# Squares in two 64-row tiles, two block rows at a time, and weight stacks in three column tiles

## The chip, the cores and the metric

The kernel runs on one core of one Trainium2 chip. The metric is device time in microseconds (us), the median of several executions. TensorE multiplies matrices and writes to the memory PSUM; VectorE and ScalarE work element by element and copy results out of PSUM; SyncE issues the transfers (DMA). "Before" drifts from chip to chip and run to run: its medians beside the different experiments were 2007.0, 2006.6, 2003.6, 2008.3 and 2000.6 us, and within the rounds of e1 to e4 its runs lie anywhere from 1998 to 2008 us. So small differences are judged by ratios within the same rounds, or by single stretches of the traces.

## The reference

A small attention block makes x from 32 inducing points; a SwiGLU FFN with an rms norm in front follows.

```python
def mab(q, kv):                       # softmax(q kv^T / sqrt(C)) kv
    ...
h = mab(I, x); y = mab(x, h)          # B=4, N=12416, m=32, C=128
rms = sqrt(mean(y*y, -1) + 1e-06)     # per row of 128
xn = y / rms * rms_g
out = (silu(xn @ w_gate) * (xn @ w_val)) @ w_out    # d_ff = 1536
```

All is float32. y = a @ h has rank 32, so the kernel never feeds y to the FFN: it multiplies the 32 attention weights `a`, scaled by 1/rms, with the "stacks" h*g*w_gate and h*g*w_val. y itself is made only to get its mean square. "a" and the stacks are each split into a rounded high part and what the rounding left, the low part: 32 rows of "a" go in as high, low, high, low against high, high, low, low of the stack, so one matmul with 128 rows sums all four products.

## The kernel before

Rows come in 97 blocks of 128 per batch. Four blocks are a unit (25 units a batch, counted from 0; the last two have three and two blocks), four units are a set. The FFN of one unit is 12 steps j. Into these steps the kernel weaves, by a fixed plan, the attention of the next batch ("attention steps") and the "seam" of a later set: transposes, squares, scale, split. Everything shares the PSUM tiles "mm", of which there are two.

```python
ps_gv = pool("ps_gv", 4, space=PSUM)
ps_acc = pool("ps_acc", 2, space=PSUM)
ps_m = pool("ps_m", 2, space=PSUM)          # the tiles "mm"
...
def square(t, rows, at):                    # one block row t of a set: 4 blocks
    k = rows // m
    ps = ps_m.tile([P, R, C], F32, name="mm", tag="mm")
    nc.tensor.matmul(ps[:, 0:k, :], st["aT"][0:rows, ts(t, P)], diag[b][0:rows, 0:k, :], ...)   # L437
    sq = work.tile([P, R, C], F32, name="sq", tag="sq")
    nc.scalar.activation(sq[:, 0:k, :], ps[:, 0:k, :], AF.Square)
    nc.vector.reduce_sum(out=st["ms"][:, ds(at // m, k)], in_=sq[:, 0:k, :], axis=AX.X)
...
def stack(i, c):                            # h*g*w, 512 columns at a time
    ps = bank()
    nc.tensor.matmul(ps[:], st["hg"][:], st.pop(("w", i, c))[:], ...)                           # L392
    ... VectorE: high part to all rows, low part to rows 64 to 127
...
for j in range(NJ):                         # ffn of one unit
    matmul g (L504); matmul v (L506); silu on ScalarE; multiply on VectorE
    if j == 4 and stores:
        stores.pop()()                      # turn_out of the unit before: transposes, copy L494, store
    slot(j)                                 # attention steps, then the seam's steps planned here
    if len(late) > 1:
        late.pop(0)()                       # project (L487) of two steps earlier
```

`diag` holds four copies of h in a block-diagonal form, so one float32 matmul with 128 rows and 512 columns gives y for four blocks; three quarters of the array's work are zeros.

Of the kernel before, what the change touches and what calls it, by code (L numbers as in the profile page):

```python
# [9 lines left out]
F32 = mybir.dt.float32  # L10
F32R = mybir.dt.float32r
I32 = mybir.dt.int32
U32 = mybir.dt.uint32
AF = mybir.ActivationFunctionType
ALU = mybir.AluOpType
AX = mybir.AxisListType
PSUM = bass.MemoryType.PSUM

P = 128
R = 4  # L20
TB = 4
GB = R * TB
# [3 lines left out]
def kernel(  # L26
# [27 lines left out]
    nc = tc.nc  # L54
    B, N, C = x.shape
    m = inducing.shape[0]
    F = moe_w_gate.shape[1]
    NB = N // P
    NJ = F // P
    NG = NB // GB  # L60
    H = P // 2
    SCALE = float(1.0 / (C ** 0.5))
    assert C == P and m * R == P and F % 512 == 0 and N % P == 0
    assert NG >= 1 and NB - NG * GB in (0, 1)


    groups = [(g * GB, GB, R, TB) for g in range(NG)]
# [15 lines left out]
    def chunks(s):  # L83

        at = 0
        for t in range(TB):
            rows = m * sum(units[u][1] > t for u in sets[s])
            if rows:
                yield t, rows, at
            at += rows  # L90
# [12 lines left out]
    def first(s):  # L103
        return units[sets[s][0]][0]

    def count(s):
        return sum(units[u][1] for u in sets[s])

    def pool(name, bufs, **kw):
        return ctx.enter_context(tc.tile_pool(name=name, bufs=bufs, **kw))  # L110
# [5 lines left out]
    small = pool("small", 2)  # L116
    work = pool("work", 3)
    once = pool("once", 1)
# [7 lines left out]
    ps_m = pool("ps_m", 2, space=PSUM)  # L126
# [15 lines left out]
    gam = const.tile([P, 1], F32, name="gam")  # L142
# [6 lines left out]
    w32 = [[dram.tile([P, 512], F32, name=f"w{i}{c}") for c in range(F // 512)] for i in range(2)]  # L149
# [14 lines left out]
    ps = ps_m.tile([P, 512], F32, name="mm", tag="mm")  # L164
# [54 lines left out]
    sc, diag, stacks = {}, {}, {}  # L219

    def attention(b, load_next):

        st = {}
        steps = []
        add = steps.append
# [7 lines left out]
        def bank():  # L233
            if b:
                return ps_m.tile([P, 512], F32, name="mm", tag="mm")
            return ps_gv.tile([P, 512], F32, name="gv", tag="gv")
# [99 lines left out]
        def end_h():  # L336
            ps = bank()
            nc.tensor.matmul(ps[:, 0:C + 1], fold[:].rearrange("p q m -> p (q m)"), st["hl"][:], start=True, stop=True)
            rec = small.tile([P, 1], F32, name="rec")
            nc.vector.tensor_scalar_add(out=rec[:], in0=ps[:, C:C + 1], scalar1=1e-9)  # L340
            nc.vector.reciprocal(out=rec[:], in_=rec[:])
            h = st["h"] = once.tile([P, C], F32, name="h")
            nc.vector.tensor_scalar_mul(out=h[:], in0=ps[:, 0:C], scalar1=rec[:])

            d = diag[b] = small.tile([P, R, C], F32, name="diag")
            nc.gpsimd.memset(d[:], 0.0)
            for q in range(R):
                nc.gpsimd.tensor_copy(out=d[ts(q, m), q, :], in_=h[ts(q, m), :])

        def turn_h():  # L350
            ps = bank()
            nc.tensor.transpose(ps[:, 0:P], st["h"][:], ident[:])
            hT = st["hT"] = once.tile([P, m], F32, name="hT")
            nc.vector.tensor_copy(out=hT[:], in_=ps[:, 0:m])
            hg = st["hg"] = once.tile([P, P], F32, name="hg")
            nc.vector.tensor_scalar_mul(out=hg[:], in0=ps[:, 0:P], scalar1=gam[:])
            stacks[b] = [stk.tile([P, F], F32R, name=n) for n in ("sg", "sv")]

        add(end_h)
# [22 lines left out]
        def exp2():  # L382
            nc.scalar.activation(sc[b][:, 0:NB * m], sc[b][:, 0:NB * m], AF.Exp, scale=SCALE)

        def fetch(i, c):
            w = st["w", i, c] = work.tile([P, 512], F32, name="w", tag="sq")
            nc.sync.dma_start(out=w[:], in_=w32[i][c][:])

        def stack(i, c):

            ps = bank()
            nc.tensor.matmul(ps[:], st["hg"][:], st.pop(("w", i, c))[:], start=True, stop=True)  # L392
            w = stacks[b][i]
            nc.vector.tensor_copy(out=w[:, ts(c, 512)], in_=ps[:])
            nc.vector.tensor_tensor(out=w[H:P, ts(c, 512)], in0=ps[H:P, :], in1=w[H:P, ts(c, 512)].bitcast(F32),
                                    op=ALU.subtract)

        for s in range(len(sets)):
            add(lambda s=s: scores2(s))
# [1 line left out]
                add(lambda s=s: turn_s(s - 1))  # L401
        add(lambda: turn_s(len(sets) - 1))
        add(exp2)
        ics = [(i, c) for c in range(F // 512) for i in range(2)]
        add(lambda: fetch(*ics[0]))
        for one, two in zip(ics, ics[1:]):
            add(lambda one=one, two=two: (fetch(*two), stack(*one)))
        add(lambda: stack(*ics[-1]))
        return steps

    def blocks(b, s):

        return sc[b][:, ds(first(s) * m, count(s) * m)].rearrange("p (j m) -> p j m", m=m)

    def seam(b, s):

        st = {}
        nb = count(s)

        def turn_a():  # L420
            ps = ps_m.tile([P, 512], F32, name="mm", tag="mm")
            for t, rows, at in chunks(s):
                nc.tensor.transpose(ps[0:rows, ts(t, P)], sc[b][:, ds(first(s) * m + at, rows)], ident[:])  # L423
            aT = st["aT"] = once.tile([P, 512], F32, name="aT")
            for r0, r1, n in rects(s):
                nc.scalar.copy(out=aT[r0:r1, 0:n], in_=ps[r0:r1, 0:n])  # L426
            l = st["l"] = small.tile([P, GB], F32, name="l")
            nc.vector.reduce_sum(out=l[:, 0:nb], in_=blocks(b, s), axis=AX.X)
            nc.vector.tensor_scalar_add(out=l[:, 0:nb], in0=l[:, 0:nb], scalar1=1e-9)
            nc.vector.scalar_tensor_tensor(out=l[:, 0:nb], in0=l[:, 0:nb], scalar=1e-6, in1=l[:, 0:nb],  # L430
                                           op0=ALU.mult, op1=ALU.mult)
            st["ms"] = small.tile([P, GB], F32, name="ms")

        def square(t, rows, at):
            k = rows // m
            ps = ps_m.tile([P, R, C], F32, name="mm", tag="mm")
            nc.tensor.matmul(ps[:, 0:k, :], st["aT"][0:rows, ts(t, P)], diag[b][0:rows, 0:k, :], start=True, stop=True)  # L437
            sq = work.tile([P, R, C], F32, name="sq", tag="sq")
            nc.scalar.activation(sq[:, 0:k, :], ps[:, 0:k, :], AF.Square)  # L439
            nc.vector.reduce_sum(out=st["ms"][:, ds(at // m, k)], in_=sq[:, 0:k, :], axis=AX.X)  # L440

        def scale():
            ms = st["ms"]
            nc.vector.scalar_tensor_tensor(out=ms[:, 0:nb], in0=ms[:, 0:nb], scalar=1.0 / C, in1=st["l"][:, 0:nb],  # L444
                                           op0=ALU.mult, op1=ALU.add)
            rs = small.tile([P, GB], F32, name="rs")
            nc.gpsimd.tensor_tensor(out=rs[:, 0:nb], in0=ms[:, 0:nb], in1=mhalf[:, 0:nb], op=ALU.pow)  # L447
            a = blocks(b, s)
            nc.gpsimd.tensor_tensor(out=a, in0=a, in1=rs[:, 0:nb].unsqueeze(2).to_broadcast((P, nb, m)), op=ALU.mult)

        def split():
            ps = ps_m.tile([P, 512], F32, name="mm", tag="mm")
            for t, rows, at in chunks(s):
                nc.tensor.transpose(ps[0:rows, ts(t, P)], sc[b][:, ds(first(s) * m + at, rows)], ident[:])  # L454
            tag = "" if len(sets[s]) == R else "s"
            hi, lo = (halves.tile([P if not tag else rects(s)[0][1], rects(s)[0][2]], F32R, name=n + tag) for n in ("hi", "lo"))
            for r0, r1, n in rects(s):
                nc.vector.tensor_copy(out=hi[r0:r1, 0:n], in_=ps[r0:r1, 0:n])
                nc.vector.tensor_tensor(out=lo[r0:r1, 0:n], in0=ps[r0:r1, 0:n], in1=hi[r0:r1, 0:n].bitcast(F32),
                                        op=ALU.subtract)  # L460
            for q, u in enumerate(sets[s]):
                split_of[b, u] = (q, hi, lo)

        return [turn_a] + [lambda c=c: square(*c) for c in chunks(s)] + [scale, split]

    split_of, moving = {}, {}

# [64 lines left out]
    for k, (b, s) in enumerate(order):  # L532
        if len(sets[s]) < R:
            continue
        following = order[k + 1:k + 3]
        if following and len(sets[following[0][1]]) < R:
            steps = seam(*following.pop(0))
            for i, f in enumerate(steps):
                plan.setdefault((b, sets[s][0], min(NJ - 1, 2 * i + 1)), []).append(f)
        if following:  # L540
            steps = seam(*following[0])
            at = [(1, 1), (1, 4), (1, 7), (1, 10), (2, 1), (2, 4), (2, 10)]
            for (n, j), f in zip(at, steps):
                plan.setdefault((b, sets[s][n], j), []).append(f)
    after = {}
# [52 lines left out]
```

## Time and profile before

| what | value |
|---|---|
| median of 3 runs | 2007.02 us |
| FFN begins | 149.3 us |

### The profile page before, as it was taken

The numbers are of one execution on the slowest core, as the hardware profiler recorded it, in microseconds if no ns is written. First come the engines' busy times: TensorE is split into PE (matmuls) and PEld (weight loads), VectorE is DVE, ScalarE is ACT, GpSimd is POOL, SyncE is SP. The second block draws the span as 40 slices with busy tenths as digits, with TensorE's granted clock in tenths as the row PEclk, the third lists the DMA queues.
The fourth block names the chain that finished last, engine by engine and source line by source line (L and its number), as shares of the span: only waits on it lengthen the run. The fifth ranks groups of instructions, "written<-read, shape, count | busy, mean of one in ns | idle before, by whom it ended". The sixth has DMA issues, their size and how long they took to land.

```text
span 2004.2 us, 22358 instructions
## 1 busy us (share of the span) xinstructions
PE 1910.3 (95%) x7445; PEld 1101.8 (55%) x7445; DVE 1170.0 (58%) x1973; ACT 910.5 (45%) x1550; POOL 116.7 (6%) x92
## 2 busy tenths in 40 slices
PE   4369999999999999999999999999999999999999
PEld 2135555555556555555556655555555655555556
DVE  3655565565756555556666656556575556556555
ACT  1114445445445444544544544544544544444544
POOL 0110000010000000000000000001000000000000
PEclk7589999999999999999999999999999999999999
DMA  5240110410201101130111010000020110111010
GB/s 185 68 167 19 33 30 19 137 44 27 64 27 29 32 22 32 59 123 22 47 38 32 25 32 29 25 28 21 27 64 27 30 32 28 36 32 32 27 33 24
DMA packets 44707, 90.35 MB, mean 45 GB/s; under 512 B 9232, under 2 KB 13360, under 8 KB 41520
## 3 DMA queue, kind: packets, MB, share of 16 engines
q1 hardware_dynamic: 44400, 88.90, 14.3%
q8 instruction: 59, 0.97, 0.2%
q14 instruction: 56, 0.46, 0.1%
q10 hardware_dynamic: 192, 0.02, 0.0%
HBM read 36.45 MB, written 27.00 MB: 32 GB/s over the span
## 4 chain that ended last, share of the span: by engine, by line
PE 91%; DVE 2%; ACT 2%; issue 1%; DMA 0%; POOL 0%; SPq 0%; ACTq 0%; POOLq 0%; DVEq 0%
PE acc L487 50%; PE gv L506 13%; PE gv L504 13%; PE mm L437 4%; PE mm L492 2%; PE mm L242 2%; PE mm L366 1%; PE mm L320 1%; PE mm L250 1%; PE mm L392 1%; PE mm L454 1%; PE mm L423 1%; ACT L508 0%; PE mm L308 0%; PE mm L375 0%
## 5 line engine op out<-in xcount | busy, mean ns | idle before, releaser
L510 DVE TENSOR_TENSOR u<-silu,gv 128x512 f32<-128x512 f32 (+2 forms) x1200 | 804.1, 671 | 707.1 <-ACT silu L508 605.5
L487 PE MATMUL acc<-u,wo 128*128 128x512 f32 (+2 forms) x2400 | 1206.1, 584 | 0.0
L508 ACT ACTIVATE silu<-gv 128x512 f32<-128x512 f32 (+2 forms) x1200 | 701.5, 585 | 836.6 <-PE gv L504 454.0
L504 PE MATMUL gv<-a,sg 128*128 128x512 f32 (+2 forms) x1200 | 930.4, 775 | 20.0 <-ACT silu L508 15.3
L487 PEld LDWEIGHTS acc<-u,wo 128*128 128x128 f32 x2400 | 426.0, 189 | 151.6 <-issue 85.9
L506 PE MATMUL gv<-a,sv 128*128 128x512 f32 (+2 forms) x1200 | 466.2, 389 | 0.0
L504 PEld LDWEIGHTS gv<-a,sg 128*128 128x128 f32 x1200 | 228.0, 190 | 298.2 <-issue 216.8
L506 PEld LDWEIGHTS gv<-a,sv 128*128 128x128 f32 x1200 | 228.7, 191 | 274.2 <-issue 197.6
L447 POOL TENSOR_TENSOR rs<-ms,mhalf 128x16 f32<-128x16 f32 (+2 forms) x28 | 71.8, 2564 | 1567.7 <-DVE ms L444 1567.7
L437 PE MATMUL mm<-diag,aT 128*128 128x512 f32 (+1 forms) x208 | 102.1, 574 | 0.8 <-ACT aT L426 0.8
L440 DVE TENSOR_REDUCE ms<-sq 128x4 f32<-128x512 f32 (+1 forms) x104 | 67.2, 649 | 39.0 <-ACT sq L439 38.7
L439 ACT ACTIVATE sq<-mm 128x512 f32<-128x512 f32 (+1 forms) x104 | 59.2, 569 | 57.3 <-PE mm L437 56.3
L499 ACT COPY oT<-acc 128x512 f32<-128x512 f32 (+2 forms) x100 | 57.3, 573 | 52.1 <-PE acc L487 51.8
L494 DVE COPY o<-mm 128x512 f32<-128x512 f32 (+2 forms) x100 | 66.8, 668 | 1.7 <-PE mm L492 1.7
L492 PE MATMUL mm<-ident,oT 128*128 128x128 f32 x388 | 58.6, 272 | 0.5 <-ACT oT L499 0.5
L492 PEld LDWEIGHTS mm<-ident,oT 128*128 128x128 f32 x388 | 48.2, 140 | 13.3 <-ACT oT L499 0.9
L242 PE MATMUL mm<-ident,xn 128*128 128x128 f32 x288 | 43.1, 272 | 0.0
L437 PEld LDWEIGHTS mm<-diag,aT 128*128 128x128 f32 (+1 forms) x208 | 36.4, 192 | 11.4 <-issue 4.9
L250 PE MATMUL gv<-xT,indT 128*32 128x512 f32 (+1 forms) x50 | 16.8, 889 | 27.0 <-DVE xT L215 25.7
L242 PEld LDWEIGHTS mm<-ident,xn 128*128 128x128 f32 x288 | 35.8, 140 | 9.3
L242 PE MATMUL gv<-ident,xn 128*128 128x128 f32 x96 | 20.4, 382 | 17.6 <-DVE xT L215 14.8
L217 ACT COPY xT<-gv 128x512 f32<-128x512 f32 x12 | 7.0, 586 | 60.2 <-PE gv L242 60.2
(145 smaller groups left out, 699.1 us busy)
## 6 DMA issues: line engine op xcount, KB each, us to landing
xn<-in_x_dram SPq DMA_DIRECT2D x24, 1024.0 KB, 6.2
out_dram<-o SPq DMA_DIRECT2D x92, 256.0 KB, 2.0
a<-hi SPq DMA_DIRECT2D x184, 64.0 KB, 2.0
a<-lo SPq DMA_DIRECT2D x184, 64.0 KB, 2.0
w<-w SPq DMA_DIRECT2D x30, 256.0 KB, 2.8
sc<-in_moe_w_gate_dram SPq DMA_DIRECT2D x3, 512.0 KB, 3.8
sc<-in_moe_w_val_dram SPq DMA_DIRECT2D x3, 512.0 KB, 4.0
sc<-in_moe_w_out_dram SPq DMA_DIRECT2D x3, 512.0 KB, 5.1
```

The costliest lines, as they stand in the source:

```text
L242: nc.tensor.transpose(ps[:, ts(t, P)], xnat[b, g][:, q * nt + t, :], ident[:])
L437: nc.tensor.matmul(ps[:, 0:k, :], st["aT"][0:rows, ts(t, P)], diag[b][0:rows, 0:k, :], start=True, stop=True)
L439: nc.scalar.activation(sq[:, 0:k, :], ps[:, 0:k, :], AF.Square)
L440: nc.vector.reduce_sum(out=st["ms"][:, ds(at // m, k)], in_=sq[:, 0:k, :], axis=AX.X)
L447: nc.gpsimd.tensor_tensor(out=rs[:, 0:nb], in0=ms[:, 0:nb], in1=mhalf[:, 0:nb], op=ALU.pow)
L487: nc.tensor.matmul(acc[:, 0:T], wo[:, j, :], t[:, 0:T], start=(j == 0), stop=(j == NJ - 1))
L492: nc.tensor.transpose(ps[:, ts(t, P)], oT[:, ts(t, P)], ident[:])
L494: nc.vector.tensor_copy(out=o[:, 0:nt, :].rearrange("p t c -> p (t c)"), in_=ps[:, 0:T])
L504: nc.tensor.matmul(g[:, 0:T], sg[:, ts(j, P)], a[:, 0:T], start=True, stop=True)
L506: nc.tensor.matmul(v[:, 0:T], sv[:, ts(j, P)], a[:, 0:T], start=True, stop=True)
L508: nc.scalar.activation(s[:, 0:T], g[:, 0:T], AF.Silu)
L510: nc.vector.tensor_tensor(out=t[:, 0:T], in0=s[:, 0:T], in1=v[:, 0:T], op=ALU.mult)
```

## The change

The squares are cut into an upper and a lower half of 64 rows: two row tiles that may run side by side, each with its own PSUM tile, two block rows per step. This halves the zeros. The stacks are no longer made with four copies of h*g as weights (128 columns) but with one (32 columns), three pieces of w side by side in three column tiles. VectorE splits the result once, and DMA puts the halves in place, 12 transfers per stack.

```diff
-            d = diag[b] = small.tile([P, R, C], F32, name="diag")
+            d = diag[b] = small.tile([P, 2, C], F32, name="diag")
...
-            hg = st["hg"] = once.tile([P, P], F32, name="hg")
+            hg = st["hg"] = once.tile([P, m], F32, name="hg")
...
+        def fetch(i):
+            st["w", i] = [work.tile([P, 512], F32, name="w", tag="sq") for c in range(NC)]
+            for w, d in zip(st["w", i], w32[i]):
+                nc.sync.dma_start(out=w[:], in_=d[:])
+        def stack(i):
+            ps = bank()
+            for c, w in enumerate(st.pop(("w", i))):
+                nc.tensor.matmul(ps[ts(c, m), :], st["hg"][:], w[:], start=True, stop=True)
...          (hi and lo on VectorE)
+            for k, half in enumerate((hi, hi, lo, lo)):
+                for c in range(NC):
+                    nc.sync.dma_start(out=stacks[b][i][ts(k, m), ts(c, 512)].bitcast(F32),
+                                      in_=half[ts(c, m), :].bitcast(F32))
...
-        ics = [(i, c) for c in range(F // 512) for i in range(2)]   (7 attention steps)
+        for i in range(2):                                          (4 attention steps)
+            add(lambda i=i: fetch(i))
+            add(lambda i=i: stack(i))
...
+        def square(*ts_):                 # two block rows
+            ps = [ps_m.tile([P, 2, 2, C], F32, name="mm", tag="mm") for h in halves_ if h]
...          (for each block row n, for each half r:)
+                        rows = ds(r * H, k * m)
+                        nc.tensor.matmul(ps[r][:, n, 0:k, :], st["aT"][rows, ts(t, P)], diag[b][rows, 0:k, :], ...)
...
-            at = [(1, 1), (1, 4), (1, 7), (1, 10), (2, 1), (2, 4), (2, 10)]
+            at = [(1, 1), (1, 4), (1, 10), (2, 4), (2, 10)]
```

In `at`, a pair (n, j) is step j of unit n of a set, n counted from 0; the squares' steps are the second and third pair now.

More of the change, by code (lines that the diff above doesn't have):

```diff
@@ L63 @@
     assert C == P and m * R == P and F % 512 == 0 and N % P == 0
-    assert NG >= 1 and NB - NG * GB in (0, 1)
+    assert NG >= 1 and NB - NG * GB in (0, 1) and F // 512 <= R
     groups = [(g * GB, GB, R, TB) for g in range(NG)]
@@ L343, in end_h @@
             nc.vector.tensor_scalar_mul(out=h[:], in0=ps[:, 0:C], scalar1=rec[:])
-            d = diag[b] = small.tile([P, R, C], F32, name="diag")
+            d = diag[b] = small.tile([P, 2, C], F32, name="diag")
             nc.gpsimd.memset(d[:], 0.0)
             for q in range(R):
-                nc.gpsimd.tensor_copy(out=d[ts(q, m), q, :], in_=h[ts(q, m), :])
+                nc.gpsimd.tensor_copy(out=d[ts(q, m), q % 2, :], in_=h[ts(q, m), :])
         def turn_h():
@@ L354, in turn_h @@
             nc.vector.tensor_copy(out=hT[:], in_=ps[:, 0:m])
-            hg = st["hg"] = once.tile([P, P], F32, name="hg")
-            nc.vector.tensor_scalar_mul(out=hg[:], in0=ps[:, 0:P], scalar1=gam[:])
+            hg = st["hg"] = once.tile([P, m], F32, name="hg")
+            nc.vector.tensor_scalar_mul(out=hg[:], in0=ps[:, 0:m], scalar1=gam[:])
             stacks[b] = [stk.tile([P, F], F32R, name=n) for n in ("sg", "sv")]
@@ L383, in exp2 @@
             nc.scalar.activation(sc[b][:, 0:NB * m], sc[b][:, 0:NB * m], AF.Exp, scale=SCALE)
-        def fetch(i, c):
-            w = st["w", i, c] = work.tile([P, 512], F32, name="w", tag="sq")
-            nc.sync.dma_start(out=w[:], in_=w32[i][c][:])
-        def stack(i, c):
-            ps = bank()
-            nc.tensor.matmul(ps[:], st["hg"][:], st.pop(("w", i, c))[:], start=True, stop=True)
-            w = stacks[b][i]
-            nc.vector.tensor_copy(out=w[:, ts(c, 512)], in_=ps[:])
-            nc.vector.tensor_tensor(out=w[H:P, ts(c, 512)], in0=ps[H:P, :], in1=w[H:P, ts(c, 512)].bitcast(F32),
-                                    op=ALU.subtract)
+        NC = F // 512
+        def fetch(i):
[3 more added lines that the diff above has]
+        def stack(i):
+            ps = bank()
+            for c, w in enumerate(st.pop(("w", i))):
+                nc.tensor.matmul(ps[ts(c, m), :], st["hg"][:], w[:], start=True, stop=True)
+            hi, lo = (work.tile([P, 512], F32R, name=n, tag="work") for n in ("whi", "wlo"))
+            rows = slice(0, NC * m)
+            nc.vector.tensor_copy(out=hi[rows, :], in_=ps[rows, :])
+            nc.vector.tensor_tensor(out=lo[rows, :], in0=ps[rows, :], in1=hi[rows, :].bitcast(F32), op=ALU.subtract)
+            for k, half in enumerate((hi, hi, lo, lo)):
+                for c in range(NC):
+                    nc.sync.dma_start(out=stacks[b][i][ts(k, m), ts(c, 512)].bitcast(F32),
+                                      in_=half[ts(c, m), :].bitcast(F32))
         for s in range(len(sets)):
@@ L403, in attention @@
         add(exp2)
-        ics = [(i, c) for c in range(F // 512) for i in range(2)]
-        add(lambda: fetch(*ics[0]))
-        for one, two in zip(ics, ics[1:]):
-            add(lambda one=one, two=two: (fetch(*two), stack(*one)))
-        add(lambda: stack(*ics[-1]))
+        for i in range(2):
+            add(lambda i=i: fetch(i))
+            add(lambda i=i: stack(i))
         return steps
@@ L432, in turn_a @@
             st["ms"] = small.tile([P, GB], F32, name="ms")
-        def square(t, rows, at):
-            k = rows // m
-            ps = ps_m.tile([P, R, C], F32, name="mm", tag="mm")
-            nc.tensor.matmul(ps[:, 0:k, :], st["aT"][0:rows, ts(t, P)], diag[b][0:rows, 0:k, :], start=True, stop=True)
-            sq = work.tile([P, R, C], F32, name="sq", tag="sq")
-            nc.scalar.activation(sq[:, 0:k, :], ps[:, 0:k, :], AF.Square)
-            nc.vector.reduce_sum(out=st["ms"][:, ds(at // m, k)], in_=sq[:, 0:k, :], axis=AX.X)
+        def square(*ts_):
+            halves_ = [[(t, min(2, rows // m - 2 * r), at // m + 2 * r) for t, rows, at in ts_ if rows // m > 2 * r]
+                       for r in range(2)]
+            ps = [ps_m.tile([P, 2, 2, C], F32, name="mm", tag="mm") for h in halves_ if h]
+            for n in range(len(ts_)):
+                for r, h in enumerate(halves_):
+                    if n < len(h):
+                        t, k, _ = h[n]
+                        rows = ds(r * H, k * m)
+                        nc.tensor.matmul(ps[r][:, n, 0:k, :], st["aT"][rows, ts(t, P)], diag[b][rows, 0:k, :],
+                                         start=True, stop=True)
+            for r, h in enumerate(halves_):
+                if not h:
+                    continue
+                sq = work.tile([P, 2, 2, C], F32, name="sq", tag="sq")
+                parts = [(slice(0, len(h)), h[0])] if len({k for _, k, _ in h}) == 1 and len(ts_[0:]) and \
+                    (len(h) == 1 or h[1][2] - h[0][2] == R) else [(slice(n, n + 1), one) for n, one in enumerate(h)]
+                for n, (_, k, at) in parts:
+                    nc.scalar.activation(sq[:, n, 0:k, :], ps[r][:, n, 0:k, :], AF.Square)
+                    count_ = n.stop - n.start
+                    to = st["ms"][:, ds(at, k)] if count_ == 1 else \
+                        st["ms"][:, ds(at - 2 * r, count_ * R)].rearrange("p (n q) -> p n q", q=R)[:, :, 2 * r:2 * r + k]
+                    nc.vector.reduce_sum(out=to, in_=sq[:, n, 0:k, :] if count_ > 1 else sq[:, n.start, 0:k, :], axis=AX.X)
         def scale():
@@ L462, in split @@
                 split_of[b, u] = (q, hi, lo)
-        return [turn_a] + [lambda c=c: square(*c) for c in chunks(s)] + [scale, split]
+        cs = list(chunks(s))
+        return [turn_a] + [lambda c=c: square(*c) for c in (cs[0:2], cs[2:4]) if c] + [scale, split]
     split_of, moving = {}, {}
```

## The prediction

> **What bounds the kernel now.** I read the page first: the engines' shares, the chain that ended last, then the costliest groups.
>
> ```profile
> PE 1910.3 (95%) x7445; PEld 1101.8 (55%) x7445; DVE 1170.0 (58%) x1973; ACT 910.5 (45%) x1550; POOL 116.7 (6%) x92
> ...
> PE 91%; DVE 2%; ACT 2%; issue 1%; DMA 0%; POOL 0%; SPq 0%; ACTq 0%; POOLq 0%; DVEq 0%
> ...
> L437 PE MATMUL mm<-diag,aT 128*128 128x512 f32 (+1 forms) x208 | 102.1, 574 | 0.8 <-ACT aT L426 0.8
> ```
>
> TensorE is the bound: 91% of the chain is its own work, and VectorE and ScalarE mostly wait for it. So every microsecond that TensorE streams less, or stands still more, goes into the time nearly whole. L437 makes y for the rms. The chain by line gives it 3.9% (78 us) and the h*g*w stacks (L392) 0.8% (16 us). These 94 us are all that the change can attack.
>
> Next, the chain of waits in a small window tells what one such product costs back to back (start, length, what).
>
> ```profile
> 345.91 0.44 PE mm L308 x4
> 346.34 0.86 PE mm L437 x2
> 347.20 0.86 PE acc L487 x2
> ```
>
> A float32 matmul of 512 columns is recorded as two and takes 0.86 us of TensorE; four transposes take 0.44. A step of the FFN loop (one j) is 0.86 + 0.23 + 0.23 = 1.32 us.
>
> Third, the timeline around a spot where the output of the unit before is turned (L492) and a square follows in the same step: it decides this case.
>
> ```profile
> 415.41 0.39 PE L506 MATMUL gv<-a,sv 128*128 128x512 f32 x1
> ...
> 415.64 0.60 PE L492 MATMUL mm<-ident,oT 128*128 128x128 f32 x4
> ...
> 416.07 1.02 PE L437 MATMUL mm<-diag,aT 128*128 128x512 f32 x2
> 416.24 0.69 DVE L510 TENSOR_TENSOR u<-silu,gv 128x512 f32<-128x512 f32 x1 [0.64 <-PE mm L492]
> ...
> 416.84 0.68 DVE L494 COPY o<-mm 128x512 f32<-128x512 f32 x1
> 416.94 1.02 PE L487 MATMUL acc<-u,wo 128*128 128x512 f32 x2
> ```
>
> The reader is to see that the square starts at 416.07 although L494 copies the transposes out only until 417.52. It can, because the "mm" buffers are two and it takes the other one.
>
> Fourth, the queue that issues the transfers, where the first "a" is gathered:
>
> ```profile
> 146.60 0.58 SPq L474 DMA_DIRECT2D a<-hi  x1
> 147.24 0.58 SPq L474 DMA_DIRECT2D a<-lo  x1
> 147.86 0.59 SPq L474 DMA_DIRECT2D a<-hi  x1
> ```
>
> A 32-partition placement costs the queue 0.63 us from one to the next, and lands 2.0 us after its issue (row a<-hi of the issues).
>
> **What the Trainium skill says.** "TensorEngine Tiling (Array Packing)", section Key Properties: tiles work independently, but a change of tiling mode drains TensorE. Section Gotcha 1 (PSUM Pressure): row tiles write to different banks. That is why the new code takes two PSUM tiles at once. The trace agrees on both properties where columns are tiled already:
>
> ```profile
> 350.76 0.39 PE L506 MATMUL gv<-a,sv 128*128 128x512 f32 x1
> ...
> 351.08 1.08 PE L320 MATMUL mm<-xn,a 128*32 128x128 f32 x32
> ...
> 352.09 1.13 PE L437 MATMUL mm<-diag,aT 128*128 128x512 f32 x2
> ```
>
> L320 is 16 float32 matmuls of 128 columns. One after the other they would need 16 x 0.86/4 = 3.4 us; they took 1.0, so four ran at once, both passes included. The price is at the edges: the stretch begins 0.32 after L506's start instead of 0.23; its end at 352.09 is 1.01 later, against 3.44/4 = 0.86; and the next float32 product lasts 1.13 instead of 1.02, its weights not loaded ahead. Together 0.35 us for one trip into another tiling and back. No row tiling side by side is in this trace, so that rows behave as columns do is taken from the page. "TensorE: Matmul & The Clock Gate", Part 3, The mechanism, says matmuls start and end in program order; so one matmul that waits holds up all behind it.
>
> **The change part by part.**
>
> Squares. There are 24 full sets of 16 blocks; one runs in the start-up and 23 inside the FFN. Before, a set has four squares of 0.86. After, it has two steps. Each step holds four matmuls with 64 rows and 256 columns, two per row tile: 2 x 0.43 = 0.86 us if the halves overlap fully. I add 0.41 for the trip (0.35 as above, a little more because these weights have 128 columns): 1.27 against 1.71 for two old squares. That saves 0.44 us a step, if nothing waits. ScalarE and VectorE process as many elements as before.
>
> But each step writes both "mm" buffers. It therefore waits until the last user of either has been copied out. I laid out the schedule by hand, from the numbers of steps (75 before, 72 after, spread over 228 slots). The first step of each set falls on j=4 of its unit, directly behind the turned output, in all 23 sets. There the second row tile's first matmul waits for the end of L494, 1.45 us after the transposes have left (416.07 to 417.52). Only the first tile's first matmul (0.43) runs meanwhile. The step lasts 1.45 + 0.05 for the semaphore + 0.11 for weights + 0.86 + 0.2 on the way out = 2.67, against 1.71: a loss of 0.96. 23 x 0.96 = +22 us. Three times (unit 17 of batches 0 to 2) an attention step with two VectorE operations of 0.69 lies between as well: 3 x 1.4 = +4. Three times (unit 1, j=10) the second step directly follows another attention step: about 1.1 worse than a free one, 3 x 0.7 over the old code = +2. The other 20 second steps are free: 20 x -0.44 = -9. The old squares had a few waits of their own (listed by line L437: 4.9 + 1.3 + 0.8), of which I count 3 as gone.
>
> Stacks inside the FFN (batches 1 to 3). Six products of 0.86 become two groups of three side by side, 0.86 + 0.33 each: 5.15 - 2.4 = -2.8 us per batch, -8 in all. VectorE drops from 12 operations of 0.69 to 4. In exchange 24 placements go through the queue, which is in order, and the weights of the second stack are fetched behind the 12 placements of the first. From the start S of the first stack: hi is ready at S+2.0, 12 x 0.63 brings S+9.6, three fetches of about 0.4 follow, and the last lands 2.8 us after its issue (row w<-w): S+13.2. TensorE arrives at the second stack after 6 steps of 1.32, 1.2 for the first stack and 0.44 for a split: S+9.6. So it stands for about 3.5 us, 3 x 3.5 = +10.
>
> Start-up (batch 0). Here nothing hides the queue. Before, the stack products run from 124.8 to 131.7 and the first set's transposes follow at once. After: first stack 124.8, hi at 127.5, 12 placements to 135, fetches landed near 138.4, second stack until 139.3, then the transposes: 7.5 us later. VectorE is freer there but then waits for ScalarE; I keep +7.
>
> Sum: 7 + 22 + 4 + 2 - 9 - 3 - 8 + 10 = +25 us, so 2007 + 25 = 2032 us.
>
> **The rivals.**
> One: the saving arrives whole. All matmul terms without waits give 46 x -0.44 - 8 = -28, some 1979 us. The 91% of TensorE on the chain speaks for it. Against it: two buffers, and a program order that puts the output's transposes just ahead of the step.
> Two: row tiles do not overlap in float32, the passes going one after the other. A free step costs 1.71 + 0.41 and a waiting one some 0.4 more: 20 x 0.86 + 26 x 0.43 = +28, some 2060 us. The column-tiled L320 speaks against it; nothing in this trace shows row tiles.
> Three: the queue hurts more. Late placements delay the next gather of "a". By my count the last placement is issued near S+23 and the gather behind it lands near S+27; "a" is needed near S+30. It just fits. A few us of delay in three batches would give 2040. In the other direction the fetch may land earlier.
> Four: ScalarE or VectorE becomes the bound because two 0.60 us squares and two 0.69 us sums now come in a bunch. I reckon the next silu is delayed by 0.1 us and its product is needed two steps later, so this costs nothing.
>
> **Range and chances.** The wait behind the output is sized from a copy that repeats almost identically, but whether part of it is absorbed I cannot see; the start-up and the fetch are worth 17 together and could be half or one and a half. Range 2008 to 2056. Faster by over 2% (below 1967) would need more than rival one: 0.03. Slower by over 2% (above 2047) needs rival two or three: 0.20. Within 2%: 0.77.
>
> **What would show it.** Right: TensorE idle time before the square's second row tile, released by L494's copy, about 1 us each at 23 places; steps at j=10 that take about 1.3 us; a wait of 3 to 4 us before each second stack, released by the transfer of w; the first FFN matmul near 156 instead of 149. Wrong: no waits at the squares (then the time falls below 2000), square steps longer than 2 us without a wait (no overlap of rows), or no wait at the second stack.

## More of the kernel before

The prediction shows the main lines. Two more are needed later: the g and v matmuls, which read "a" and the stacks. The columns are count, busy us, mean ns of one, then idle time before.

```profile
L504 PE MATMUL gv<-a,sg 128*128 128x512 f32 x1104 | 875.1, 793 | 20.0 <-ACT silu L508 15.3 <-DMA a<-lo 4.7
L506 PE MATMUL gv<-a,sv 128*128 128x512 f32 x1104 | 436.3, 395 | 0.0
```

The reader is to note the mean durations, 793 and 395 ns.

## The result, and the profile after

The changed kernel takes 2051.21 us (2050.51 to 2052.26, 4 runs), the kernel before in the same rounds 2006.57. The ratio is 1.0226 with a 95% interval of 1.0209 to 1.0244: slower. Ratios here are the mean time of one kernel's runs over that of the other's of the same rounds, so they are not quite the ratio of the medians. Executions over 1.5% slower than the fastest of the same kernel are left out of the means.

The page of the changed kernel: engines, chain, and the squares, now L451.

```profile
PE 1916.0 (93%) x7637; PEld 1104.7 (54%) x7637; DVE 1145.2 (56%) x1945; ACT 904.6 (44%) x1554; POOL 115.7 (6%) x92
...
PE 88%; DVE 3%; issue 2%; ACT 2%; DMA 1%; SPq 0%; POOL 0%; ACTq 0%; POOLq 0%; DVEq 0%
...
L451 PE MATMUL mm<-diag,aT 64*128 64x256 f32 (+1 forms) x400 | 77.3, 403 | 20.5 <-DVE o L519 17.1
```

TensorE's share of the chain fell from 91 to 88%, and VectorE, DMA and "issue" rose: the end now waits more. The squares are busy for 77.3 us instead of 102.1, so that part of the intent came true. Most of what they save is spent in idle time (20.5 us), 17.1 us of it until "o" (L519, the copy of the turned output) is done.

The chain of waits in unit 1 of the last batch, where no attention step disturbs (start, length, what):

```profile
1643.42 0.45 PE mm L517 x4
1643.87 0.02 DVE u L535
1643.89 0.57 issue
1644.46 0.69 DVE o L519
1645.15 0.04 issue
1645.19 1.13 PE mm L451 x6
1646.32 1.06 PE acc L512 x2
...
1654.47 1.06 PE mm L451 x8
1655.54 1.06 PE acc L512 x2
```

The turned output's transposes end at 1643.87. The chain then goes over to VectorE, and comes back to the squares (L451) at 1645.19, when the copy is out. Only six of the eight recorded passes lie behind the wait; the first row tile's first matmul ran ahead. The second step, at 1654.47, waits for nothing: its four matmuls, which one after the other would need 4 x 0.43 = 1.72 us by the prediction's figures, take 1.06 us, so the row tiles do run side by side. The project behind it takes 1.06 instead of 0.86, taken here for the way back to full tiling. From the starts of successive g matmuls in the trace, the j step with a free pair of squares lasts 2.59 us where a plain one lasts 1.32, so a free step costs 1.27. The one behind the output lasts 4.43 where the same with the output alone lasts 1.76, so it costs 2.67.

The second place is the second stack. The timeline of the changed kernel around it, first batch (queue SP, then TensorE):

```profile
539.29 3.67 SPq L404 DMA_DIRECT2D sg<-whi  x6
...
543.06 3.70 SPq L404 DMA_DIRECT2D sg<-wlo  x6
...
546.86 1.50 SPq L390 DMA_DIRECT2D w<-w  x3
...
549.97 3.60 PE L397 MATMUL mm<-w,hg 128*32 128x512 f32 x6 [2.92 <-DMA w<-w]
```

The 12 placements of the first stack hold the queue from 539.3 to 546.8, and only then are the weights of the second stack fetched. TensorE, done with its v matmul at 547.05, stands until 549.97, and then needs 3.60 us for three matmuls that took 1.06 in the first stack. The next view tells part of the reason; it lists busy time by engine in a stretch, then the granted TensorE clock (1.00 is full speed), then DMA.

```profile
546.80:549.90 3.10, 0.24 (x2) 0.00 (x0) 2.70 (x5) 0.60 (x1) 0.00 (x0) 1.00 0.72 204
549.90:553.60 3.70, 3.63 (x7) 0.57 (x7) 0.00 (x0) 0.00 (x0) 0.00 (x0) 0.65 0.23 75
```

After the wait the granted clock averages 0.65, and the three pieces of w arrive one by one, so the column tiles do not run side by side. Which of the two counts more, the other two batches tell:

```profile
1037.65 2.35 PE L397 MATMUL mm<-w,hg 128*32 128x512 f32 x6 [2.93 <-DMA w<-w]
...
1524.96 2.81 PE L397 MATMUL mm<-w,hg 128*32 128x512 f32 x6 [2.81 <-DMA w<-w]
...
1037.70:1041.50 3.80, 3.80 (x11) 1.33 (x12) 1.38 (x2) 0.17 (x1) 0.00 (x0) 1.00 0.16 59
```

TensorE stood as long there, but the granted clock stayed at 1.00 (in the third batch too), and the three matmuls still took 2.35 and 2.81 us. So the pieces that arrive one by one cost 1.3 to 1.8 us every time, and the slow clock came on top in one of three batches. The Trainium skill's "TensorE: Matmul & The Clock Gate", Part 1, What's actually happening, says that an idle window of about 3.4 us halves the clock. The halving agrees (the granted clock is 0.50 from 551.1 to 554.4); the idle time does not, since 2.92 us were enough here, while 2.93 and 2.81 us had no such effect.

The start-up, in the same timeline:

```profile
133.53 1.50 SPq L390 DMA_DIRECT2D w<-w  x3
...
136.58 3.46 PE L397 MATMUL gv<-w,hg 128*32 128x512 f32 x6 [12.40 <-DMA w<-w]
...
157.19 0.77 PE L529 MATMUL gv<-a,sg 128*128 128x512 f32 x1 [4.74 <-DMA a<-lo]
```

The same order on the queue makes TensorE wait 12.4 us, and the FFN begins at 157.2 instead of 149.3. This start varies from execution to execution: e3 below has the same start-up code and begins at 160.3. Counted from the first stack product (124.81 before, 123.12 after), the start-up grew by 9.6 us; the attention before it happened to end 1.7 us earlier in this execution.

The third finding I had not thought of. In the last batch no stack is made and no attention runs, and yet a plain unit there lasts 16.34 us instead of 16.24. The g and v matmuls of the changed kernel:

```profile
L529 PE MATMUL gv<-a,sg 128*128 128x512 f32 x1104 | 882.6, 799 | 21.0 <-ACT silu L533 16.3 <-DMA a<-lo 4.7
L531 PE MATMUL gv<-a,sv 128*128 128x512 f32 x1104 | 440.5, 399 | 0.6 <-DVE u L535 0.5
```

They last 799 and 399 ns instead of 793 and 395. A few ns twice in each of 1200 steps make several us.

### The profile page after: what moved, and what is told of

The parts are those of the page before. It is cut to its first block, busy times and chain, and to the rows that moved or that the text cites. A ratio compares the mean times of both kernels' runs of the same rounds, so it can differ in the third digit from the quotient of the medians.

```text
span 2049.5 us, 22880 instructions
## 1 busy us (share of the span) xinstructions
PE 1916.0 (93%) x7637; PEld 1104.7 (54%) x7637; DVE 1145.2 (56%) x1945; ACT 904.6 (44%) x1554; POOL 115.7 (6%) x92
## 4 chain that ended last, share of the span: by engine, by line
PE 88%; DVE 3%; issue 2%; ACT 2%; DMA 1%; SPq 0%; POOL 0%; ACTq 0%; POOLq 0%; DVEq 0%
PE acc L512 49%; PE gv L529 13%; PE gv L531 13%; PE mm L451 3%; PE mm L517 2%; PE mm L242 2%; PE mm L366 1%; PE mm L320 1%; PE mm L250 1%; DVE o L519 1%; ACT silu L533 1%; PE mm L430 1%; PE mm L478 1%; DMA w<-w 1%; PE mm L397 1%
## 5 line engine op out<-in xcount | busy, mean ns | idle before, releaser
L529 PE MATMUL gv<-a,sg 128*128 128x512 f32 (+2 forms) x1200 | 938.1, 782 | 21.0 <-ACT silu L533 16.3
L451 PE MATMUL mm<-diag,aT 64*128 64x256 f32 (+1 forms) x400 | 77.3, 403 | 20.5 <-DVE o L519 17.1
L464 DVE TENSOR_REDUCE ms<-sq 128x4 f32<-128x512 f32 (+2 forms) x108 | 63.0, 626 | 51.2 <-ACT sq L460 51.2
L460 ACT ACTIVATE sq<-mm 128x512 f32<-128x512 f32 (+2 forms) x108 | 53.7, 551 | 70.3 <-PE mm L451 69.5
L451 PEld LDWEIGHTS mm<-diag,aT 64*128 64x128 f32 (+1 forms) x400 | 44.1, 185 | 48.7 <-DVE o L519 25.7
L519 DVE COPY o<-mm 128x512 f32<-128x512 f32 (+2 forms) x100 | 66.7, 667 | 1.7 <-PE mm L517 1.7
```

Source lines behind the costliest of these rows:

```text
L451: nc.tensor.matmul(ps[r][:, n, 0:k, :], st["aT"][rows, ts(t, P)], diag[b][rows, 0:k, :], start=True, stop=True)
L464: nc.vector.reduce_sum(out=to, in_=sq[:, n, 0:k, :] if count_ > 1 else sq[:, n.start, 0:k, :], axis=AX.X)
L519: nc.vector.tensor_copy(out=o[:, 0:nt, :].rearrange("p t c -> p (t c)"), in_=ps[:, 0:T])
L529: nc.tensor.matmul(g[:, 0:T], sg[:, ts(j, P)], a[:, 0:T], start=True, stop=True)
```

## The experiments

Main theory: the squares' first step waits for the output's copy because it wants both "mm" tiles; the second stack waits because its fetch queues behind the placements. Rivals: row tiles do not overlap, or cost their mode change too dearly; the placements themselves are the burden. All kernels were correct.

**e1: the squares alone** (stacks and their 75 steps as before).

> Only the squares of the change, at the slots of the change; stacks as before (75 attention steps). Main theory (the first step of each set waits for the copy of the turned output, a free step costs about 1.27 us): 23 x +0.96 = +22, 20 free second steps x -0.44 = -9, three second steps behind an attention step +2, old waits -3: +12 us, about 2019. Rival (row tiles do not overlap): +40 us, about 2047. Rival (squares are all of the loss but the start-up): about 2043.

Measured: 2022.92 us, ratio 1.0094 (1.0070 to 1.0119). This is +19 against the 2003.6 of the same rounds, a little above the forecast +12 and far from the no-overlap rival's +40. In the trace most sets of squares (its step behind the output and its free step, against four old squares) cost 0.5 us more than before, as 2.67 + 1.27 - 3.44 = 0.50 says. The excess is in unit 17 of three batches, some 4 to 5.5 us each: there the large exp of ScalarE sits two steps ahead, with the 1.28 us that ScalarE then takes to load a table for the next silu, VectorE's copy waits behind it, and the squares behind the copy. TensorE stands for 5.2 us there, and the granted clock is 0.50 for some 6.8 us from 980.7 on.

**e2: the stacks alone** (squares as before).

> Only the stacks of the change; squares as before. Main theory: start-up +8 us; in each of batches 1 to 3 a wait for the second stack's weights behind 12 placements, with its matmuls then one by one on a slow clock, about +6.2, less 2.8 of saved TensorE work: +10. Together +18, about 2025. Rival (the long unit 18 comes from exp2 and the squares having moved next to each other, not from the fetch): +8 only, about 2015.

Measured: 2035.33 us, ratio 1.0159 (1.0134 to 1.0184), +32 against 2003.6. Both the main theory (+18) and its rival (+8) gave too little. The FFN begins at 157.9 us (+8.6), units 17 and 18 together are 4.7 to 6.2 us longer, and every plain unit of the last batch is 16.34 or 16.35 us. So the 0.10 us a unit comes with the stacks and not with the squares: in e1 the unit is 16.24 us.

**e3: the first square step at j=5**, one step behind the output.

```diff
-            at = [(1, 1), (1, 4), (1, 10), (2, 4), (2, 10)]
+            at = [(1, 1), (1, 5), (1, 10), (2, 4), (2, 10)]
```

> The changed kernel with the first square step one slot later (j=5 in place of j=4), so that the output's copy is done by then. Main theory (wait for the copy): 23 x -1.4 = -32, a few us back for new neighbours (max3, h sum): about 2020. Rival (row tiles cost that much by themselves, with the drain of the mode change): no change, 2051.

Measured: 2028.61 us, ratio 1.0116 against the changed kernel's 1.0226. The chain in unit 1 of the last batch:

```profile
1627.56 0.43 PE mm L517 x4
...
1629.32 1.14 PE mm L451 x8
1630.46 1.05 PE acc L512 x2
```

The transposes, one FFN step, then the squares with nothing between. In the trace the four batches are 7.9, 3.0, 8.1 and 6.6 us shorter than in the changed kernel; the second is short of the rest because its unit 18 lasted 31.29 us instead of 28.55. The wait for w there was no longer (2.89 us), but the granted clock was 0.50 for about 6.8 us twice (from 1007.7 and from 1028.2), in the changed kernel once for 3.4 us (from 1018.7). The forecast of about 2020 was missed by 9 us: besides this batch, the start-up took 3.2 us more, which the edit does not touch. In the last batch, 6.6 us over five sets is 1.33 us a set (2.67 - 1.27 = 1.40 was expected). The wait is shown as the cause, and the rival, that the tiling itself costs that much, has fallen.

**e4: the second stack's fetch ahead of the placements.**

```diff
+            if i == 0:
+                fetch(1)
             for k, half in enumerate((hi, hi, lo, lo)):
...
-            add(lambda i=i: fetch(i)) / add(lambda i=i: stack(i))   for i in 0, 1
+        fetch(0), stack(0), an empty step, stack(1)
```

> The changed kernel with the second stack's three fetches put on the queue ahead of the first stack's 12 placements; same steps, same squares. Main theory: the 12.4 us wait in the start-up goes (first FFN matmul near 148 in place of 157, -9 us) and so do three waits of about 6.2 us: -28, about 2023. Rival (the placements themselves, their traffic or their landing, cause the delay): within 5 us of 2051.

Measured: 2028.35 us, ratio 1.0119. The timeline of the first batch's stacks:

```profile
531.59 1.06 PE L397 MATMUL mm<-w,hg 128*32 128x512 f32 x6
...
532.67 1.27 SPq L390 DMA_DIRECT2D w<-w  x3
...
534.03 3.68 SPq L406 DMA_DIRECT2D sg<-whi  x6
...
541.16 1.06 PE L397 MATMUL mm<-w,hg 128*32 128x512 f32 x6
```

The fetch is issued before the placements, and the second stack takes 1.06 us without a wait. Unit 18 falls from 29.87, 28.55 and 28.90 us to 24.00, 23.93 and 23.87, that is 5.2 us a batch (6.2 was expected); the FFN begins at 151.0 instead of 157.2, 6 us earlier instead of 9. All 24 placements are still there, so the order on the queue is the cause, not the placements.

**e5: old stacks, first square step at j=5** (e1 with e3's edit).

> Stacks as before, squares of the change, first step at j=5 instead of j=4. Main theory: the first steps become free (23 x -1.4 = -32) and the three steps behind exp2, which cost about 3 us more than the others in the run with squares alone, lose that too: 2023 - 32 - 9 = 1982 to 1990 where before is 2004 to 2007, a ratio near 0.99. Rival (row tiles side by side save nothing): not below 2004.

Measured: 2003.95 us, ratio 0.9986 (0.9969 to 1.0004): no gain, a miss. The last batch is right, 419.15 us against 423.14 before, 0.8 us a set. But unit 17 of the first two batches is still 28.9 and 28.7 us (25.3 and 23.7 before; 22.2 in e3, where the exp falls into unit 18). The timeline there:

```profile
975.66 2.79 ACT L383 ACTIVATE sc<-sc 128x3104 f32<-128x3104 f32 x1
...
981.34 3.06 PE L444 MATMUL mm<-diag,aT 64*128 64x256 f32 x8
981.59 0.69 DVE L512 COPY o<-mm 128x512 f32<-128x512 f32 x1
```

The exp (L383) stops ScalarE, hence VectorE, hence the copy of the output, which is not out before 982.28. So at j=5 the squares still wait for it, and then run on a slowed clock (granted 0.50 from 981.3). Moving a step by one place in the program is not moving it by one place in time.

**e6: the stacks alone, hg at its old size.** The stacks' edit made the tile hg 384 bytes a partition shorter, so every tile allocated behind it moved, "a" among them.

```diff
-            hg = st["hg"] = once.tile([P, m], F32, name="hg")
+            hg = st["hg"] = once.tile([P, P], F32, name="hg")[:, 0:m]
```

> Stacks alone as in the earlier run, but the tile hg is allocated at its old size (512 bytes a partition, of which 128 are used), so that all tiles allocated after it keep their old addresses. In that run each FFN unit was 0.10 us longer than before, in all batches, although no stack is made in the last. Address theory: the 0.10 us a unit goes, about -8 us, near 2027 where the unpadded was 2035. Rival (stacks written by transfers and not by VectorE are slower to read, or it is the chip's state): 2035.

Measured: 2029.98 us, ratio 1.0117 against e2's 1.0159. Plain units of the last batch are 16.24 us again. The v matmuls of this run:

```profile
L513 PE MATMUL gv<-a,sv 128*128 128x512 f32 x1104 | 436.4, 395 | 0.7 <-DVE u L517 0.7
```

395 ns, as before, with the placements all there.

**e8: the kernel before, shifted.** Nothing but 128 unused bytes a partition behind hg.

```diff
-            hg = st["hg"] = once.tile([P, P], F32, name="hg")
+            hg = st["hg"] = once.tile([P, P + m], F32, name="hg")[:, 0:P]
```

> The kernel before with nothing changed but hg's tile 128 bytes a partition longer, unused, so that later tiles move by 128 bytes; the changed kernel moved them by -384, which is the same modulo 512. Address theory: each plain FFN unit goes from 16.24 to 16.34 us, about +8 us in all. Rival: no change.

Measured: 2011.19 us, ratio 1.0023 (1.0007 to 1.0039). Plain units of the last batch: 16.34 or 16.35 us. The v matmuls:

```profile
L506 PE MATMUL gv<-a,sv 128*128 128x512 f32 x1104 | 439.1, 398 | 0.0
```

So a shift of addresses alone does it: the profile is 5.6 us longer, 8 us was expected. Which of the tiles matters is not settled. By the order of allocation in the kernel the stacks come ahead of hg and do not move; "a", the moving operand of exactly the two matmuls that grew, does; the float32 projects, whose operand "u" moves too, keep their spacing. I take "a" for the cause, but no run moved it alone.

**e7: the changed kernel with all three cures** (e3, e4 and the old size of hg).

> The changed kernel with all three cures: first square step at j=5, second stack's fetches ahead of the placements, hg at its old size. Sum of the single effects: 2051 - 31 - 23 - 8 = about 1990. Rival (the cures overlap, since one wait hides in another): above 2000.

Measured: 1990.12 us (1985.15 to 1994.32), ratio 0.9917 (0.9897 to 0.9937). It beats both kernels, by 0.8% over before and about 3% over the change as it came, and it lies where the sum of the single effects put it.

**e9 and e10: two refinements.** e9 is e5 with the first square step of unit 17 at j=7; e10 is e7 with the second step at j=7.

```diff
-            at = [(1, 1), (1, 5), (1, 10), (2, 4), (2, 10)]
+            at = [(1, 1), (1, 7 if s == 4 else 5), (1, 10), (2, 4), (2, 10)]     # e9
+            at = [(1, 1), (1, 5), (1, 7), (2, 4), (2, 10)]                       # e10
```

> The kernel with old stacks and the first square step at j=5, but in unit 17 at j=7. There the step took 4.61 us at j=5, because the copy of the output that it waits for is in VectorE's queue behind work that waits for the large exp of j=2. Theory: in unit 17 the step falls to about 2.7 us; unit 17 of batches 0 to 2 from 28.9, 28.7 and 27.5 us to about 26; in all -6 to -9 us against the earlier run (2004), so 1995 to 1998. Rival (the exp itself, not the wait on its queue, costs the time): no change, 2004.

> The kernel with all three cures, and the second square step at j=7 instead of j=10, away from the attention step that shares j=10 in unit 1 of three batches: 3 x -0.7 us there, up to 0.2 us back at units 1 and 5, where an attention step is one slot earlier: about -1 us against the earlier 1990, inside the spread of the runs.

e9 measured 1996.43 us, ratio 0.9968 (0.9949 to 0.9987). Unit 17 fell to 26.57, 26.55 and 26.54 us, 1.0 to 2.3 us less each; that the squares stood on the exp's tail is confirmed in the trace, with 5.4 us in all a little under the 6 to 9 told. The two ratios alone (0.9968, and 0.9986 for e5) would not show it, as their intervals overlap. e10 measured 1995.56 us, ratio 0.9962 (0.9944 to 0.9981). Unit 1 gained the 0.7 us as told (21.15 to 21.16 after 21.80 to 21.83), but unit 9 lost 1.25 us (24.75 after 23.50), and by the ratios, taken in different rounds, it is no better than e7 (0.9917), rather worse. The forecast of about -1 us was missed.

## Why the prediction was right or wrong

The direction and the range (2008 to 2056) held; the middle of it, +25 us, was 20 us short, and I gave "slower by over 2%" only 0.20. That the result lies in the range is in part luck: its upper part stood for rivals two and three, and neither came. By its own steps, with the profiled spans (2004.2 before, 2049.5 after, +45.3):

| step | predicted | measured | from |
|---|---|---|---|
| start-up | +7 | +7.9 | first FFN matmul, 149.3 to 157.2 |
| stacks inside the FFN | -8 + 10 = +2 | about +12.4 | e6: batches 0 to 2 against before, 4.46 + 4.58 + 3.35 |
| squares | +22 + 4 + 2 - 9 - 3 = +16 | about +19 | the rest; e1's four batches give 18.9 |
| addresses | none | +5.6 | e8 against before |

- The free step of 1.27 us and the waiting one of 2.67: measured 1.27 and 2.67. The wait behind L494 is at 23 places, as told, and e3 takes it away.
- The start-up: the cause was right; that the size fits (7.5 worked out, 7.9 measured) is in part luck. The wait came as told, but the second stack, counted there as one group of three side by side (0.9 us), took 3.46 us, the same omission as in the next point. An attention that ended 1.7 us earlier hid most of it.
- The step that failed is "so it stands for about 3.5 us, 3 x 3.5 = +10". The mechanism was right, e4 removes it; the term was mis-sized. TensorE did stand for about 3 us. But I ended the cost there. The three matmuls then took 3.60, 2.35 and 2.81 us instead of 1.06, since the pieces of w come one by one; in the first batch the clock was down as well, and the project behind them took 1.57 instead of 1.02. That is about 3 + 2.5 + 0.6, some 6 us, in the first batch and 4.3 to 4.7 in the others, 15 in all instead of 10; e4 got back 5.2 a batch. The 12.4 of e6 against the predicted 2 is 10 us, half of what was missing. In e6 this step (unit 18, j=11) lasts 6.81, 8.50 and 7.36 us where it lasts 2.51 without the wait (e7), again 15 us in all, so 5 of the 10 us are found. The other 5 are not split and stay open: the attention steps shift against the squares as well.
- Missing altogether: the address term. Shrinking hg looked free.
- The squares' remaining +3 is not taken apart. One part shows: the prediction took all 24 sets for 16 blocks, but the last full set of each batch has 15, and its second step makes the j step 3.00 us instead of 2.59. In the last batch of e1, units 17 and 18 with this set are 1.1 us longer than before where other sets are 0.5 longer; if the other batches are like it, that is some 2.5 us in four batches. That the old waits counted as gone (-3) did not go is not shown. The 18.9 of e1 is no proof of the 19: its excess in unit 17 comes from the exp, which lies in unit 18 in the changed kernel.
- The rivals: row tiles do overlap in float32 (eight passes in 1.06 us; rival two fell with e1 and e3). Rival one's saving exists, once the waits are moved: in the last batch, e5 gains 0.8 us a set. Late gathers of "a" (rival three) do not show: the g matmuls wait 4.7 us for "a" in both kernels, once, at the start. A bound ScalarE or VectorE (rival four) does not show either: the g matmuls' waits for silu are 15.3 us before and 16.3 after.

## What to carry to other kernels

A step that takes all buffers of a ring waits for the slowest reader of each of them, so place it where the neighbours ahead of it have been copied out, and check that place in time, not in program order, wherever a long instruction can hold the copying engine up. On an in-order transfer queue a fetch that TensorE will wait for goes ahead of bulk placements; and if what it fetches comes in pieces that were to run side by side, count them as run one after the other. A wait near three microseconds may be paid a second time in a slow clock, here behind the second stack in one batch of three. When a tile changes size, look whether matmuls that have nothing to do with it changed their duration.

## What the Trainium skill lacked or had wrong

- "TensorEngine Tiling (Array Packing)", Key Properties: that a change of mode drains TensorE is right, but it has no size. Here a free step in two row tiles costs 1.27 us where the overlapped streaming is 0.86: about 0.41 us for the trip there and back.
- The same page, Theoretical Speedup: "Up to 2x" for row tiles. For two pairs of float32 matmuls with 64 rows and 256 columns between full-array work, the step fell from 1.71 to 1.27 us, a factor of 1.35, for that reason.
- "DMA: Bandwidth & Descriptors", Issuing engines are not separate DMA queues: the time to start a transfer is called usually small relative to the transfer. Here one 64 KB placement costs the queue 0.63 us of the 2.0 us from its issue to its landing, 12 of them 7.5 us, and this order held TensorE up for 12.4 us once and about 3 us three times.
- "SBUF — State Buffer", Operand start alignment: it asks only for a multiple of the element size, and that is all correctness needs here too. It says nothing of time: 128 bytes of shift took the v matmuls from 395 to 398 ns and the kernel 0.23% up (e8).
- "TensorE: Matmul & The Clock Gate", Part 1, What's actually happening: an idle window of about 3.4 us is named for the half clock. Here shorter standstills were enough, 2.92 us in the changed kernel (at 547.0) and 2.70 us in the kernel before (at 813.1), each followed by a granted clock of 0.50 for about 3.4 us; others of 2.93 and 2.81 us (at 1034.7 and 1522.2) were not followed by it.
